# The last two chunks of tokens cut at 448 and 256 columns in place of 320 and 384, in a fused attention and expert kernel

## The chip, the cores and the metric

The kernel runs on one core of a Trainium2 chip. The metric is the device time of one execution in microseconds. The trace names the engines PE (matmul), PEld (its weight loads), DVE, ACT, POOL and SP (which issues most DMAs); each works through its own queue in order, and semaphores hold an instruction until what it needs is there.

## The reference

```python
# attention: q, k, v of (4, 4, 1088, 32); S1, S2 of (8, 32)
phi = lambda x: outer(S1 @ x, S2 @ x)               # 64 features per row
kv, z = phi(k).T @ v, phi(k).sum(rows)
attn = (phi(q) @ kv) / (phi(q) @ z + 1e-6)
x = attn, heads side by side                        # (4352 tokens, 128)
# four experts: w1 of (4, 128, 1024), w2 of (4, 1024, 128)
p = domain_probs / (domain_probs.sum(-1) + 1e-9)
out = sum over e of p[:, e:e+1] * (relu(x @ w1[e]) @ w2[e])
```

All inputs and the output are float32.

## The kernel before

**Two halves that overlap.** The attention produces the token matrix x piece by piece (generator `front`, cut into units of up to 576 tokens by `UNITS`); the experts consume it in ten chunks of tokens, `CHUNKS`, of 128, 448, six of 512, then 320 and 384 columns. A chunk has 32 slots (four experts of eight blocks of 128 hidden units); the first has 16. The main loop (L1468) goes through the slots in order and, between the work of the slots, calls `work`, which advances the attention by a few pieces. Before a chunk begins its tokens must be there; the last unit of the attention is complete before the next-to-last chunk starts.

**How many pieces a call of `work` advances** is decided while the program is built: a rate from the tokens still missing, a credit, and two estimates of the engines' load (`vector_time`, `scalar_time`, with LIMIT and SLOT).

**One slot.** Float32 accuracy is made of three float32r products, so a block takes six PE passes of the chunk's width: wa and wb into an h bank (`opening`, L1126 to L1137), then wd into the same bank one slot later (`third`, L1154), after ACT has scaled the bank in place (L1135); then va, vb and vd into an o bank (`second`, five slots later by LAG, four in the last expert by LAG_TAIL; the vd passes are dealt out later still by `pay`). Nearly all of these passes are issued from one helper, `swap`, so they stand under L949 and are told apart by their operands. Between the two groups the hidden block is split: ACT makes ha (L1184) and, for some blocks, hc (L1186), DVE makes hb (L1191), and POOL or DVE finishes hc (L1213, L1214, L1193, L1206). A letter per block (`MAKERS`, one row per chunk; `MAKER_TAIL` for the very last expert) says which engine does what. In the letters A and N, ACT has two operations behind the scaling, in most others one.

**One expert.** After its eighth block ACT scales the o bank (L1268). When the last vd pass is in, `gather` multiplies by the expert's gate (L1396; L1394 for the first expert) and adds to the chunk's total (L1397), which sets the o bank free. There are two o banks, so the expert after the next needs it. `next_gates` then has SP load a gate (L429), a tile of 128 partitions by the chunk's width, into the buffer that has come free. After the fourth expert `turn_back` transposes the total and stores it. Six more PSUM banks are shared by everything else.

**The last chunk** ends differently: the blocks with letters X and T of its last expert are plain (`w_tail`, and L1343 after ACT's relu in L1170 and the gate in L1171), `last_sums` adds what was gathered (L1329, L1332, one addition per 128 columns), and `last_rows` turns the result by matmuls (L1343, L1346), copies it out of PSUM and stores it in two DMAs (L1353).

**SP's queue** carries the loads and stores of both halves in program order. Early on (slot 5) it stores the gates, then loads the first GATES of them, then issues `load_k(1)` and `load_v(1)` for the next batch (L1530 to L1534).

```python
    TAIL = 4
    LAG_TAIL = 4
    DEALT = (0, 1, 1, 2, 2, 2)
    PLACES += [(START[m], START[m + 1], ring, (m - 3) % 3 * CW) for m in range(3, NC)]
```

The first of these is the number of plain blocks whose weights are loaded for the last expert, the last says where in the ring of tokens a chunk lies.

Of the kernel before, what the change touches and what calls it, by code (L numbers as in the profile page):

```python
# [24 lines left out]
def kernel(  # L25
# [24 lines left out]
    nc = tc.nc  # L50
    scalar_copy = lambda to, of: nc.scalar.activation(to, of, ACTF.Copy)

    P = 128
    HP = 64
    B, H, S, D = q.shape
# [10 lines left out]
    CW = 512  # L66
    GE = 160
    LAG = 5
    GATES = 2
    BUFFERS = (7, 6, 13)  # L70
    HA, HB, HC = BUFFERS
    WHOLE = 5
# [6 lines left out]
    LAG_TAIL = 4  # L79
    DEALT_TAIL = (1, 1, 2)  # L80
    DEALT = (0, 1, 1, 2, 2, 2)
    LIMIT = 1300.0
    LIMIT_A = 1e9
    SLOT_A = 1500.0
    SLOT = 1600.0
    PLAIN = (2,)
    TOKENS_AT = 16
    AHEAD = 13
    TOKENS = 6
    LEAD = 6  # L90
    SETTLE = 1
    SPREAD = 2
    XD_BY = 'PPVVPPPVPP'
    Q_BY = 'PVPPPPVVPVVVPVVPPP'
    O_BY = 'AAAA'
    FETCH = 8
    HOLD = (3, 1)
    DELAY = 0
# [7 lines left out]
    TOKENS_BY = "VV"  # L106
    UNITS = [[P, 448, 512], [576, 512], [576, 512], [576, 512]]

    CHUNKS = [P, 448] + [512] * 6 + [320, 384]
    NC = len(CHUNKS)  # L110
    START = [sum(CHUNKS[:m]) for m in range(NC + 1)]
    assert all(sum(u) == S for u in UNITS) and sum(CHUNKS) == B * S

# [32 lines left out]
    def load_k(b):  # L146
        kn[b] = lpool.tile([P, S], F32, tag="rows", name="kn")
        load_rows(k, b, kn[b])
# [29 lines left out]
    def xpieces(name, t):  # L178
        return mpool.tile([P, 3, CW], t, tag="x", name=name)
# [235 lines left out]
    def parts(m):  # L415

        c, end, at = START[m], START[m] + CHUNKS[m], 0
        while c < end:
            n = min(end, (c // S + 1) * S) - c
            yield c // S, c % S, n, at  # L420
            c, at = c + n, at + n
# [3 lines left out]
    def load_gates(m, experts):  # L425
        for e in experts:
            gate[m, e] = mpool.tile([P, CW], F32, tag="gate", bufs=GATES, name="gate")
            for b, c, n, at in parts(m):
# [99 lines left out]
    def key_sum(b, p, kv, t0=0, n=NT):  # L528
        for t in range(t0, t0 + n):
            both(  # L530
                kv[:, 256 * p : 256 * p + 2 * (D + 1)],
                kps[b][:, t, p, :],
                vx[:, t, 2 * p : 2 * p + 2].rearrange("p h d -> p (h d)"),

                start=(p == t == 0),
                stop=(t == NT - 1),
                skip_group_check=True,
            )
# [275 lines left out]
    def queries_by_dram(b, c, n):  # L814

        for _ in range(FETCH):
            yield
# [7 lines left out]
        if c + n < S:  # L825
# [3 lines left out]
            if c + n + m == S and b < B - 1:  # L829
                load_k(b + 1)  # L830
        for _ in range(14 - FETCH):
            yield
# [118 lines left out]
    def token_parts(m):  # L951

        n = CHUNKS[m]
        t = xpieces("xs", F32R)
# [11 lines left out]
    def start():  # L966
# [37 lines left out]
        for t0, n0 in ((0, 4), (4, 5)):  # L1004
            for p in range(2):
                key_sum(b, p, kv, t0, n0)
        qp = [xd_ for xd_ in (mpool.tile([P, CW], F32, tag="gate", bufs=GATES, name="qp") for _ in range(2))]
        for x in range(2):
# [24 lines left out]
    def front():  # L1033
        for b in range(B):
            if b:
                yield from keys(b)
                if b + 1 < B:
                    load_v(b + 1)
            c = 0
            for n in UNITS[b]:  # L1040
                if b or c:
                    yield from queries(b, c, n)
                c += n
# [5 lines left out]
    slots = [("pair", 0, e, f) for e in range(E) for f in range(NP)]  # L1049
    for m in range(1, NC):  # L1050
        slots += [("one" if m > 1 or FB * e + k >= MIXED else "mixed" if FB * e + k >= WHOLE else "whole", m, e, k) for e in range(E) for k in range(FB)]
    first_slot = {m: min(i for i, s in enumerate(slots) if s[1] == m) for m in range(NC)}
    per_chunk = {m: sum(s[1] == m for s in slots) for m in range(NC)}
# [40 lines left out]
    def opening(i):  # L1094

        kind, m, e, k = slots[i]
        n = CHUNKS[m]
        if kind == "pair":
# [121 lines left out]
    def second(i):  # L1220
# [25 lines left out]
        elif kind == "one":  # L1246
# [19 lines left out]
            elif k == FB - 1:  # L1266
                if O_BY[e] == "A":
                    nc.scalar.activation(o[:, 0:n], o[:, 0:n], ACTF.Copy, scale=1.0 + R12)  # L1268
# [133 lines left out]
                yield  # L1402
            turn_back(m, total.pop(m)[:, 0:n])

    vector_time, scalar_time = [0.0], [0.0]

    def on_vector(inst):

        if inst.engine == mybir.EngineType.DVE and inst.outs:
            n = 1  # L1410
            for _, d in list(inst.outs[0].ap)[1:]:
                n *= d
            vector_time[0] += n / 0.96 + 80
        elif inst.engine == mybir.EngineType.Activation and inst.outs and type(inst).__name__ != "InstDMACopy":
            n = 1
            for _, d in list(inst.outs[0].ap)[1:]:
                n *= d
            scalar_time[0] += n * 0.834 + 50

    start()  # L1420
    nc.push_inst_callback(on_vector)
    pieces = front()
    done, credit = [0], [0]

    def piece():
        done[0] += 1
        next(pieces, None)


    needed, columns, count = [0] * NC, UNITS[0][0], 0  # L1430
    for b in range(B):
        count += 17 if b else 0
        for n in UNITS[b] if b else UNITS[0][1:]:
            count, columns = count + (20 if count else 18), columns + n
            for m in range(NC):
                if columns - n < START[m] + CHUNKS[m] <= columns:
                    needed[m] = count
    for i in range(3):
        begun_hp[i] = psum(ps_h, "h")
        half_columns(i, begun_hp[i], 0)  # L1440
# [25 lines left out]
        due.setdefault(first_slot[1] + HOLD[1] if held else i + (LAG_TAIL if final(*s[1:3]) else lag[s[0]]), []).append(i)  # L1466
    i = 0
    while i < len(slots) or i <= max(due) or owed:  # L1468
        vector_time[0] = max(0.0, vector_time[0] - (SLOT * CHUNKS[slots[i][1]] / CW if i >= first_slot[1] and i < len(slots) else 900.0))
        scalar_time[0] = max(0.0, scalar_time[0] - (SLOT_A * CHUNKS[slots[i][1]] / CW if i >= first_slot[1] and i < len(slots) else 900.0))  # L1470
        if i < len(slots):
            kind, m, _, _ = slots[i]
            at = i - first_slot[m]
            while have[0] < START[m] + CHUNKS[m]:
                piece()

            gone = START[m] + CHUNKS[m] * at / per_chunk[m]
            left = lambda c: START[c] - (CHUNKS[c - 1] * AHEAD / per_chunk[c - 1] if c > 1 else 0) - gone
            rate = CHUNKS[m] / per_chunk[m] * max(
                [0] + [(needed[c] + (LEAD if c > 1 else 4) - done[0]) / left(c) for c in range(m + 1, NC) if left(c) > 0]  # L1480
            )

            def work(share):

                if not first_slot[1] <= i < first_slot[1] + 4:
                    credit[0] = min(credit[0] + rate * share, 3)
                while credit[0] >= 1 and vector_time[0] < LIMIT and scalar_time[0] < LIMIT_A:
                    credit[0] -= 1
                    piece()

            opening(i)
            if kind == "pair":
                work(0.5)
        for j in due.get(i, ()):
            second(j)
        if SETTLE:
            settle()
        third(i - DELAY if i < len(slots) else i)
        if not SETTLE:
            settle()  # L1500
        pay()
        next(ending, None)
        if i < len(slots):
            work(0.5 if kind == "pair" else 1)
            if at == per_chunk[m] - AHEAD and 0 < m < NC - 1:
                while have[0] < START[m + 1] + CHUNKS[m + 1]:
                    piece()
            for gen in to_part.get(i, ()):
                next(gen, None)
            if m == NC - 2 and at == per_chunk[m] // 2:  # L1510
                while have[0] < B * S:
                    piece()
                w2_tail = load_tail()
                one = dram.tile([P, P], F32, name="one")
                nc.sync.dma_start(one[:, :], unit[:, 0:P])
                nc.sync.dma_start(bass.AP(one.tensor, one.offset, [[P + 1, P], [1, 1]]), unit[:, P : P + 1])
                nc.sync.dma_start(unit[:, 0:P], one[:, :])
            if i == first_slot[1] + 10:
                for j in range(3):
                    load_plain(j)  # L1520
            for j in range(3, len(plain_order)):
                if i == first_slot[2] + 8 * (j - 3) + 7:
                    load_plain(j)
            if i == first_slot[4]:
                unit = cpool.tile([P, P + 1], F32, tag="dp", name="unit")
                nc.gpsimd.memset(unit[:, 0:P], 0.0)
                nc.gpsimd.memset(unit[:, P : P + 1], 1.0)
            if i == 2:
                gate_quotients()
            elif i == 5:  # L1530
                store_gates()
                next_gates(GATES)
                load_k(1)
                load_v(1)  # L1534
        if i == 2:

            made_hp[3] = psum(ps_h, "h")
            for c in (0, HP):
                half_columns(3, made_hp[3], c)
        i += 1  # L1540
    for _ in ending:
        pass
    last_rows(NC - 1, unit)
    nc.pop_inst_callback()

# [1 line left out]
_INS = ["q", "k", "v", "S1", "S2", "moe_domain_probs", "moe_w1", "moe_w2"]  # L1547
# [26 lines left out]
```

## Time and profile before

| | us |
|---|---|
| median of 3 runs | 425.93 (425.80 to 425.94) |
| the profiled execution | 426.43 |
| its span, first to last instruction | 424.70 |
| busy: PE, ACT, DVE, POOL | 416.5, 382.0, 357.0, 355.3 |

The granted TensorE clock is 1.00 over the whole span. A busy time is the union of the records of an engine. Records of one engine overlap (an operation's record ends after the next one has started), so the distance between two starts, not the length of a record, says how fast an engine gets through its queue. A window view gives the busy time of each engine in a stretch, and the chain is the sequence of work that ended last, followed back from the end of the window.

### The profile page before, as it was taken

The page shows a single profiled execution, that of the slowest core. Times are in us where ns is not written, and L with a number is a line of the kernel's source. Part 1 is how long each engine was busy: PE and PEld are TensorE (multiplying, and loading weights), DVE is VectorE, ACT ScalarE, POOL GpSimd, SP SyncE. Part 2 cuts the span into 40 slices and gives each one's busy share as a digit, 9 for nine tenths or more (in the row PEclk, how much of TensorE's full clock was granted, in tenths as well). Part 3 has the DMA queues.
Part 4 walks back from the last instruction along what each step waited for, and adds up shares of the span by engine and source line. Part 5 has one row for each costly group of instructions (what it writes and reads, how often), then busy time and mean ns, then how long its engine had stood idle before and what let it go on. Part 6 is the DMA issues. An engine that isn't in the chain of part 4 may idle for free.

```text
span 424.7 us, 8812 instructions
## 1 busy us (share of the span) xinstructions
PE 416.5 (98%) x2819; PEld 351.7 (83%) x2819; DVE 357.0 (84%) x626; ACT 382.0 (90%) x818; POOL 355.3 (84%) x371
## 2 busy tenths in 40 slices
PE   9999999999999999999999999999999999999996
PEld 7886677888888887878888887878778888989995
DVE  5869999888798896898799996896897878879894
ACT  4368898999999998999999988998999999999992
POOL 6441468999999999997999998897989999799992
PEclk9999999999999999999999999999999999999999
DMA  6925250446512401643602415212621221040110
GB/s 194 320 60 130 47 145 2 98 80 158 165 40 51 126 27 44 136 99 95 176 5 61 114 26 117 61 33 62 161 32 23 41 75 35 23 82 27 34 38 19
DMA packets 57646, 34.66 MB, mean 82 GB/s; under 512 B 34945, under 2 KB 50689, under 8 KB 57601
## 3 DMA queue, kind: packets, MB, share of 16 engines
q1 hardware_dynamic: 57504, 34.01, 31.5%
q8 instruction: 22, 0.36, 0.4%
q14 instruction: 24, 0.19, 0.2%
q10 hardware_dynamic: 96, 0.10, 0.1%
HBM read 28.94 MB, written 5.15 MB: 80 GB/s over the span
## 4 chain that ended last, share of the span: by engine, by line
PE 82%; ACT 8%; DVE 4%; issue 3%; DMA 2%; SPq 0%; DVEq 0%; ACTq 0%
PE o L949 36%; PE h L949 36%; PE h L318 6%; ACT ha L1184 3%; ACT h L1135 3%; ACT hc L1186 2%; PE h L497 1%; DMA qn_first<-in_q_dram 1%; PE o L318 1%; DMA kn<-in_k_dram 1%; PE h L1121 1%; DVE hb L1191 1%; DVE o L1396 1%; SPq L171 0%; DVE qs L637 0%
## 5 line engine op out<-in xcount | busy, mean ns | idle before, releaser
L1214 POOL TENSOR_TENSOR hc<-hb,hc 128x512 fp32r<-128x512 f32 (+3 forms) x204 | 252.5, 1260 | 23.1 <-DVE hb L1191 16.9
L1191 DVE SCALAR_TENSOR_TENSOR hb<-h,ha 128x512 fp32r<-128x512 f32 (+3 forms) x266 | 166.8, 641 | 48.9 <-ACT hc L1186 16.9
L1135 ACT ACTIVATE h<-h 128x512 f32<-128x512 f32 (+3 forms) x283 | 166.3, 588 | 4.1 <-PE h L949 3.5
L1184 ACT ACTIVATE ha<-h 128x512 fp32r<-128x512 f32 (+3 forms) x252 | 148.8, 590 | 2.0 <-PE h L949 0.4
L949 PE MATMUL h<-xs,wd 128*128 128x512 f32 (+3 forms) x283 | 109.2, 386 | 1.3 <-ACT h L1135 0.5
L949 PE MATMUL h<-xs,wa 128*128 128x512 f32 (+3 forms) x283 | 105.5, 373 | 0.0
L949 PE MATMUL h<-xs,wb 128*128 128x512 f32 (+3 forms) x283 | 102.5, 362 | 0.0
L949 PE MATMUL o<-ha,va 128*128 128x512 f32 (+3 forms) x266 | 96.8, 364 | 1.1 <-DVE total L1397 1.1
L949 PE MATMUL o<-hb,vb 128*128 128x512 f32 (+3 forms) x266 | 96.6, 363 | 0.0
L949 PE MATMUL o<-hc,vd 128*128 128x512 f32 (+3 forms) x262 | 79.7, 366 | 0.2
L1186 ACT ACTIVATE hc<-h 128x512 fp32r<-128x512 f32 (+3 forms) x124 | 74.1, 598 | 0.0
L949 PEld LDWEIGHTS h<-xs,wd 128*128 128x128 f32 x283 | 53.3, 188 | 19.8 <-ACT h L1135 11.6
L1213 POOL TENSOR_SCALAR hc<-ha 128x512 fp32r<-128x512 f32 (+3 forms) x80 | 57.4, 717 | 8.1 <-ACT ha L1184 1.6
L949 PEld LDWEIGHTS h<-xs,wa 128*128 128x128 f32 x283 | 53.5, 189 | 9.5 <-issue 2.9
L949 PEld LDWEIGHTS h<-xs,wb 128*128 128x128 f32 x283 | 53.5, 189 | 5.7 <-issue 0.6
L949 PEld LDWEIGHTS o<-ha,va 128*128 128x128 f32 x266 | 50.3, 189 | 7.5 <-PE h L949 2.3
L949 PEld LDWEIGHTS o<-hc,vd 128*128 128x128 f32 x262 | 48.5, 189 | 7.9 <-issue 1.6
L949 PEld LDWEIGHTS o<-hb,vb 128*128 128x128 f32 x266 | 50.3, 189 | 5.5 <-DVE hb L1191 0.2
L1193 DVE SCALAR_TENSOR_TENSOR hc<-ha,hb 128x512 fp32r<-128x512 f32 (+2 forms) x41 | 36.2, 882 | 1.4
L1268 ACT ACTIVATE o<-o 128x512 f32<-128x512 f32 (+3 forms) x33 | 18.4, 557 | 0.0
L1397 DVE TENSOR_TENSOR total<-o,total 128x512 f32<-128x512 f32 (+3 forms) x26 | 16.9, 650 | 0.9
L1396 DVE TENSOR_TENSOR o<-o,gate 128x512 f32<-128x512 f32 (+3 forms) x26 | 16.8, 647 | 0.3 <-PE o L949 0.3
(161 smaller groups left out, 405.2 us busy)
## 6 DMA issues: line engine op xcount, KB each, us to landing
w_sb<-in_moe_w_dram SPq DMA_DIRECT2D x8, 512.0 KB
gate<-gates SPq DMA_DIRECT2D x16, 256.0 KB
kn<-in_k_dram SPq DMA_DIRECT2D x4, 544.0 KB
gate<-gates SPq DMA_DIRECT2D x8, 224.0 KB
qs<-rows SPq DMA_DIRECT2D x6, 288.0 KB
qs<-rows SPq DMA_DIRECT2D x12, 144.0 KB
qn<-in_q_dram SPq DMA_DIRECT2D x3, 544.0 KB
vx<-in_v_dram SPq DMA_DIRECT2D x48, 32.0 KB
```

Source lines behind the costliest of these rows:

```text
L318: nc.tensor.matmul(out(s), weights(s), moving(s), **flags)
L949: nc.tensor.matmul(to, weights, t, **flags)
L1135: nc.scalar.activation(g, g, ACTF.Copy, scale=1.0 + R12)
L1184: nc.scalar.activation(ha, g, ACTF.Relu, scale=NEAR)
L1186: nc.scalar.activation(hc, g, ACTF.Relu, scale=NEAR * R12)
L1191: nc.vector.scalar_tensor_tensor(out=hb, in0=g, scalar=0.0, in1=high, op0=ALU.max, op1=ALU.subtract)
L1193: nc.vector.scalar_tensor_tensor(out=hc, in0=high, scalar=-R12, in1=rest, op0=ALU.mult, op1=ALU.add)
L1213: nc.gpsimd.tensor_scalar(out=hc, in0=high, scalar1=R12, scalar2=1.0, op0=ALU.mult, op1=ALU.mult)
L1214: nc.gpsimd.tensor_tensor(out=hc, in0=rest, in1=both_, op=ALU.subtract)
L1268: nc.scalar.activation(o[:, 0:n], o[:, 0:n], ACTF.Copy, scale=1.0 + R12)
L1396: nc.vector.tensor_tensor(out=o[:, 0:n], in0=o[:, 0:n], in1=g, op=ALU.mult)
L1397: nc.vector.tensor_tensor(out=total[m][:, 0:n], in0=o[:, 0:n], in1=total[m][:, 0:n], op=ALU.add)
```

## The change

The next-to-last chunk becomes 448 columns wide in place of 320, the last one 256 in place of 384; together they are 704 as before. Three gate buffers are held in place of two. The rule by which a call of `work` decides how many pieces to advance is replaced by a string of digits, one for each call. Everything that the width of the last chunk sets goes with it: its slots, its output, the number of additions in L1332 and of matmuls in L1343 and L1346.

```diff
-    GATES = 2
+    GATES = 3
...
-    LIMIT = 1300.0
-    LIMIT_A = 1e9
-    SLOT_A = 1500.0
-    SLOT = 1600.0
...
-    LEAD = 6
...
+    PIECES = "01101101110110003011011011101101000012121212121111220022111110212102211121022111211101111100030111021111100021111111111111003011110210211100301111021111110012111100210211002111111020111100121111021101110030111101201011000210110020101100201010100000000000000000000000000000000000000000000000000000000000000000000000000000"
...
-    CHUNKS = [P, 448] + [512] * 6 + [320, 384]
+    CHUNKS = [P, 448] + [512] * 6 + [448, 256]
...
-            gone = START[m] + CHUNKS[m] * at / per_chunk[m]
-            left = lambda c: START[c] - (CHUNKS[c - 1] * AHEAD / per_chunk[c - 1] if c > 1 else 0) - gone
-            rate = CHUNKS[m] / per_chunk[m] * max(
-                [0] + [(needed[c] + (LEAD if c > 1 else 4) - done[0]) / left(c) for c in range(m + 1, NC) if left(c) > 0]
-            )
-
-            def work(share):
-
-                if not first_slot[1] <= i < first_slot[1] + 4:
-                    credit[0] = min(credit[0] + rate * share, 3)
-                while credit[0] >= 1 and vector_time[0] < LIMIT and scalar_time[0] < LIMIT_A:
-                    credit[0] -= 1
+            def work():
+
+                steps[0] += 1
+                for _ in range(int(PIECES[steps[0] - 1])):
                     piece()
```

What is left out removes the two estimates and their callback, and the arguments of the calls of `work`.

More of the change, by code (lines that the diff above doesn't have):

```diff
@@ L1403, in gather @@
             turn_back(m, total.pop(m)[:, 0:n])
[L1405 to L1418, printed above, removed]
     start()
-    nc.push_inst_callback(on_vector)
     pieces = front()
-    done, credit = [0], [0]
+    steps = [0]
     def piece():
-        done[0] += 1
         next(pieces, None)
[L1430 to L1437, printed above, removed]
     for i in range(3):
@@ L1468 @@
     while i < len(slots) or i <= max(due) or owed:
-        vector_time[0] = max(0.0, vector_time[0] - (SLOT * CHUNKS[slots[i][1]] / CW if i >= first_slot[1] and i < len(slots) else 900.0))
-        scalar_time[0] = max(0.0, scalar_time[0] - (SLOT_A * CHUNKS[slots[i][1]] / CW if i >= first_slot[1] and i < len(slots) else 900.0))
         if i < len(slots):
@@ L1492 @@
             if kind == "pair":
-                work(0.5)
+                work()
         for j in due.get(i, ()):
@@ L1503 @@
         if i < len(slots):
-            work(0.5 if kind == "pair" else 1)
+            work()
             if at == per_chunk[m] - AHEAD and 0 < m < NC - 1:
@@ L1543 @@
     last_rows(NC - 1, unit)
-    nc.pop_inst_callback()
 _INS = ["q", "k", "v", "S1", "S2", "moe_domain_probs", "moe_w1", "moe_w2"]
```

## The prediction

> **What bounds the kernel now.** I read the page's busy times first, then the windows view cut at the starts of the last two chunks (the first 320-column pass of L949 starts at 353.29, the first 384-column one at 383.68), then the chain of waits in those windows, and last the timeline for the distance between starts.
>
> ```profile
> PE 416.5 (98%) x2819; PEld 351.7 (83%) x2819; DVE 357.0 (84%) x626; ACT 382.0 (90%) x818; POOL 355.3 (84%) x371
> ```
>
> PE is never long idle, so a change pays only through work taken from PE, gaps in front of PE, or what comes after its last pass. But a busy PE says little: a 320-column matmul is recorded as 0.30 us long while the next one starts 0.136 us later, so a small gap hides under the overlap. I therefore count starts.
>
> ```profile
> core 0: us, PE busy (x) PEld busy (x) DVE busy (x) ACT busy (x) POOL busy (x), PEclk, DMA share, GB/s
> 305.80:353.30 47.50, 47.31 (x241) 39.49 (x241) 39.92 (x63) 47.05 (x94) 44.02 (x39) 1.00 0.23 52
> 353.30:383.70 30.40, 29.81 (x194) 27.58 (x193) 24.92 (x50) 30.23 (x86) 26.67 (x33) 1.00 0.21 45
> 383.70:418.60 34.90, 34.80 (x210) 33.16 (x209) 31.07 (x59) 32.58 (x81) 30.42 (x35) 1.00 0.12 28
> 418.60:424.70 6.10, 2.19 (x19) 2.00 (x17) 1.72 (x5) 0.56 (x2) 0.00 (x0) 1.00 0.09 32
> ```
>
> In the 320-column chunk (second row) ACT is busy 30.23 of 30.40 us; in the 384-column chunk it has 2.3 us to spare. The chain through those two windows, in the same order, says the same: only in the first does it leave PE often.
>
> ```profile
> by line: PE o L949 28.6%; PE h L949 22.2%; issue 10.6%; DVE hb L1191 9.8%; ACT ha L1184 9.5%; ACT hc L1186 7.2%; ACT h L1135 7.0%; DVE hc L1193 2.6%; DVE o L1396 2.0%; ACT xs L886 0.5%; DVEq L1362 0.2%; DVE total L1397 0.1%; DVEq L1191 0.1%
> by line: PE h L949 47.1%; PE o L949 42.6%; ACT ha L1184 4.0%; ACT h L1135 2.9%; issue 2.1%; ACT hc L1186 1.9%; ACT hid L1197 0.1%; ACTq L1135 0.0%
> ```
>
> **The two rates.** In stretches without a gap, the timeline has PE starts 0.2157 us apart at 512 columns (345.89 to 347.40, seven passes), 0.1623 at 384 (394.77 to 396.88, thirteen) and 0.136 at 320 (364.04 to 366.08, fifteen). That is one line, 0.000415 us a column plus 3 ns, and gives 0.189 at 448 and 0.109 at 256. ACT's closest starts are about 0.475, 0.37 and 0.32 us apart at 512, 384 and 320 columns: 0.427 at 448 and, carried on, 0.267 at 256. So a pass has almost no fixed part, while an ACT operation has some 50 ns that do not shrink.
>
> ```profile
> 361.88 0.44 ACT L1184 ACTIVATE ha<-h 128x320 fp32r<-128x320 f32 x1
> 362.20 0.45 ACT L1186 ACTIVATE hc<-h 128x320 fp32r<-128x320 f32 x1
> 362.51 0.46 ACT L1135 ACTIVATE h<-h 128x320 f32<-128x320 f32 x1
> ```
>
> These three are ACT's unit of work here: its records are 0.44 to 0.46 long, its starts 0.32 apart.
>
> **Part 1, PE's own work.** The next-to-last chunk costs 32 slots x 6 passes = 192 passes of its width. The last costs 96 into h, 28 blocks x 3 passes and two plain float32 blocks at the price of four passes each: 188 up to the end of w_tail. 128 columns move from the second to the first: 192 x 0.0531 = +10.20, 188 x 0.0531 = -9.98, so +0.2 us. Instruction counts do not change, except behind the last pass.
>
> **Part 2, the chunk that grows.** Before, in 353.3 to 383.7 PE starts 169 passes of 320 (23.0 us) and 24 of 512 (5.2): 28.2 of 30.4 us, 2.2 lost. The gaps between starts name them. 0.25 at 358.56 and 0.57 at 366.08 are first va passes waiting until L1397 has released an o bank. About 1.0 us in all at 372.8, 379.2 and 380.2 is a wd pass waiting for ACT's h; about 0.5 at 373.9 and 381.4 is an hc pass just behind ACT's o copy. ACT's load explains the last two: the maker letters give 84 operations, 85 with the xs split, x 0.32 = 27.2 us against 192 x 0.136 = 26.1 of PE. At 448 the same 85 cost 36.3 and PE 36.3: the 1.1 us of excess is gone, and the time from wb to the wd that needs ACT's result, eight passes at least, grows from 1.09 to 1.51 us. The bank waits should go, since the bank is needed five and thirteen slots into the chunk and the last 512-column gathers ahead of it do not grow. Bounds for what stays lost: 0.3 (only gaps that no rate explains) and 2.2 (nothing improves). The nearest row is the 512-column chunk just ahead, 47.5 us with ACT 47.05 busy, whose gaps between starts come to about 1.6 of 47.5; scaled to 37 us, 1.2; with the bank waits gone I take 1.0. Change: -1.2 (0 to -1.9). What moves with it: xs of this chunk is 448 wide at the end of the chunk ahead (+0.1 us on ACT and DVE, +0.3 on POOL), and the other one as much narrower.
>
> **Part 3, the chunk that shrinks.** Before: 180 passes and the plain blocks at 384 (30.5) and 25 passes of 320 (3.4) are 33.9 of 34.9 us, 1.0 lost. ACT: 75 x 0.373 = 28.0 against 30.5. At 256: 75 x 0.267 = 20.0 against 188 x 0.109 = 20.6, so ACT's 8% of spare time becomes 3%, and the eight passes between wb and wd are 0.87 us, against about 0.75 that ACT needs to return h (a 0.27 us matmul, 0.38 as the 128x256 rows of L1116 last, two hand-overs of some 0.05). In the last group of eight, which runs with LAG_TAIL 4, the o bank is wanted two slots after the last hc pass; two gathers of about 0.43 and one L1191 of 0.42 no longer fit, 0.4 against 0.145 now. Bounds for the loss: 0.5, if all of it stays hidden, and 3.3, if to the 1.0 of now each slot with three ACT operations (eight of 32) adds 0.15 (0.80 of ACT against six passes), the three o copies 0.8 and the bank wait 0.3. Nearest row: the 320-column chunk, 1.4 without its bank waits where ACT stood 4% above PE. With ACT 3% below, but less room to wait in, I take 1.7: change +0.7 (-0.5 to +2.3).
>
> [...]
>
> **Part 4, behind the last pass.**
>
> ```profile
> 418.79 0.57 DVE L1329 TENSOR_TENSOR h<-h,gate 128x384 f32<-128x384 f32 x1 [0.62 <-PE h L949]
> 419.39 0.86 DVE L1332 TENSOR_TENSOR hid<-h,total 128x128 f32<-128x128 f32 x3
> 420.42 0.68 ACT L51 ACTIVATE ob<-h 128x128 f32<-128x128 f32 x2 [3.57 <-PE h L1346]
> 421.13 0.60 SPq L1353 DMA_DIRECT2D out_dram<-ob  x1
> ```
>
> This is a chain: product with the gate, one addition per 128 columns, L1346, the last copy, the store. At 256 columns L1329 is 0.13 shorter (1.04 ns a column, from 0.57 at 384 and 0.69 for L1396 at 512) and one of three additions goes (0.24 between starts). The four L1343 records less (0.43) lie beside it. The store moves a third less in the 0.9 us in which the DMA view has it moving; the rest of its 3.6 us is issue and completion: -0.2. Together -0.6 (-0.35 to -0.85).
>
> **Part 5, no time.** PIECES: following the old credit rule call for call through the 320 calls of work gives the same 320 digits, 215 pieces, so the order of the attention work stays, and since all of it is done before the next-to-last chunk the new widths do not meet it. GATES: each load still follows one gather and waits for that gather's product, as the waits of SP's queue show before too (L429 on L1396, 127.6 us). The third buffer puts one more load in front of load_k(1), 0.34 us of SP at 33.9; kn is first read at 52.97, and the vx loads that follow end at 48.8 while their reader starts at 72.3. Without that cover it would cost the 0.34 and its 224 KB.
>
> **Sum.** +0.2 - 1.2 + 0.7 - 0.6 = -0.9 us. The profiled execution took 426.43 (span 424.70 and 1.73 around it), 0.5 above the median of the runs, 425.93; what is saved is within one execution, so I take it off the median: 425.0.
>
> **Rivals.** (A) Better: the wider chunk keeps only 0.3 to 0.6, the narrow one runs as densely as the 384 one does from 390 to 411: -1.7 + 0 + 0.2 - 0.6, some 423.8, at best 422.9. For it: letters with fewer ACT operations (75 against 84) sit in the narrow chunk, as its rate wants. Chance 0.20. (B) The two chunks trade evenly, +0.8 more in the last one: 425.9. Chance 0.10. (C) Slower: ACT becomes the bound of the last chunk, with the full 3.3 lost there, while the wider chunk sheds only its bank waits: +2.3 - 0.8 + 0.2 - 0.6 = +1.1, 427.0, and 427.8 where it sheds nothing. It decides if ACT's starts at 256 columns lie more than 20.6/75 = 0.274 us apart or h returns later than 0.87 us after wb; my 0.267 and 0.75 are near. Chance 0.24, and 0.01 more for the price of the page above: about +6.7 where 0.7 stood, 431. (D) A pass of 256 columns is held to its weight load: the loads are recorded as 189 ns, and 188 x 0.080 = 15 us would be 440. Against it: loads overlap at 320 columns, and L497's records, each with a 128x128 load of its own, start 0.112 apart (16 in 1.95 us). Chance 0.03.
>
> **How the numbers follow.** The forecast has 0.42. A measurement of this kernel can tell about 0.2%, 0.85 us, from no change, so its own range, 424.2 to 425.7, lies on both sides of 425.08: 0.30 of it counts as faster, 0.12 as same. Faster 0.30 + 0.20 = 0.50; same 0.12 + 0.10 = 0.22; slower 0.24 + 0.01 + 0.03 = 0.28. The range goes from the best of (A), 422.9, to the far end of (C), 427.8.
>
> **What would show it.** Right: starts 0.189 and 0.109 apart in dense stretches; the 448 chunk without the two long va gaps and about 38.1 us long (37.1 of passes, the 24 of 512 among them); about 27 us from the first 256-column pass to the last w_tail pass; 5.5 us behind it. Wrong: wd passes waiting for L1135 in most slots of the last chunk, L949 starts at 256 further apart than 0.11 with no engine to blame, gaps in the 448 chunk like those of the 320 one, or any stage before 345 us that moves.

## The result and the profile after

The changed kernel takes 427.16 us (median of nine, 426.72 to 427.49) against 425.93 (425.70 to 426.58): a ratio of 1.0028, with a 95% interval of 1.0018 to 1.0038. It is 1.2 us slower, where 0.9 us faster was forecast. The execution that was profiled took 427.38 us with a span of 425.30, so 2.08 around the span; before it was 426.43, 424.70 and 1.73. Lines behind the edit stand four lower than before: the passes of L949 are L945 now, L1135 is L1131, L1184 and L1186 are L1180 and L1182, L1191 and L1193 are L1187 and L1189, L1396 and L1397 are L1392 and L1393. In the experiments some of them shift by a few lines more.

The page's busy times after:

```profile
PE 417.3 (98%) x2813; PEld 352.2 (83%) x2813; DVE 358.1 (84%) x625; ACT 383.1 (90%) x817; POOL 355.6 (84%) x371
```

The windows after, cut at the same places (the first pass of 448, the first of 256, the first L1339):

```profile
core 0: us, PE busy (x) PEld busy (x) DVE busy (x) ACT busy (x) POOL busy (x), PEclk, DMA share, GB/s
305.70:353.15 47.45, 47.20 (x240) 39.48 (x239) 39.86 (x63) 47.00 (x94) 44.02 (x38) 1.00 0.20 51
353.15:391.60 38.45, 38.30 (x194) 35.56 (x192) 30.81 (x51) 38.27 (x86) 33.56 (x34) 1.00 0.16 39
391.60:419.70 28.10, 27.31 (x209) 25.97 (x209) 26.77 (x59) 25.85 (x81) 23.88 (x35) 1.00 0.10 24
419.70:425.30 5.60, 1.77 (x13) 1.38 (x11) 1.34 (x4) 0.28 (x1) 0.00 (x0) 1.00 0.07 23
```

Up to the start of the second row (353.15, before 353.29) nothing has moved but the whole sequence, by 0.14 us to the front. The next-to-last chunk is 8.06 us longer than before, the last one 6.81 shorter, what lies behind it 0.51 shorter: together with the 0.14 the span grew by 0.60.

Read the third row across. By their records PE, DVE, ACT and POOL are all busy for 24 to 27 of 28.1 us. Before, in the last chunk, DVE had 3.8 us to spare (31.07 of 34.90); now it has 1.3, less than ACT's 2.2. The chain through the two chunks, in the same order, puts DVE ahead of ACT as well:

```profile
by line: PE o L945 43.9%; PE h L945 41.0%; issue 7.3%; DVE hb L1187 4.0%; DVE xs L887 2.3%; DVE o L1392 1.6%; DVE total L1393 0.1%; DVE hc L1189 0.1%
by line: PE h L945 22.9%; PE o L945 22.1%; DVE hb L1187 16.0%; issue 13.9%; ACT ha L1180 8.2%; ACT h L1131 5.7%; DVE total L1393 3.8%; DVE o L1392 3.2%; ACT hc L1182 2.6%; DVE hc L1189 1.3%; DVE ha L1184 1.2%; DVE hc L1202 0.9%; DVEq L1187 
```

The wide chunk's chain is now nearly all PE, as hoped. But the last chunk's, 90% PE before and without a single DVE entry, spends 26% on DVE's L1187, L1393, L1392, L1189, L1184 and L1202 and 17% on ACT.

**How the loss is counted below.** "Gaps" are the distances between PE starts beyond the pass's own (0.110 us at 256 columns, 0.189 at 448), where they exceed it by 0.03, added up; the plain float32 passes of w_tail, which start twice as far apart (0.216 at 256 columns, 0.322 at 384), count as no gap. Before: 2.39 in the next-to-last chunk and 0.99 in the last. After: 1.46 and 2.66. Of the 2.66, 1.18 stands in front of va passes, 0.49 in front of vb, 0.37 at hc passes, 0.35 at wa and 0.27 at wd.

Where the largest of them comes from can be read in the timeline after, around one of the three va waits, and at three operations of DVE's L1189 (start, length, engine, line, operation, what ended the idle time before it):

```profile
401.14 0.83 DVE L1189 SCALAR_TENSOR_TENSOR hc<-ha,hb 128x256 fp32r<-128x256 f32 x1
...
402.22 0.62 DVE L1392 TENSOR_TENSOR o<-o,gate 128x448 f32<-128x448 f32 x1
...
402.87 0.62 DVE L1393 TENSOR_TENSOR total<-o,total 128x448 f32<-128x448 f32 x1
...
403.11 0.28 PE L945 MATMUL h<-xs,wb 128*128 128x256 f32 x1
...
403.64 0.35 PE L945 MATMUL o<-ha,va 128*128 128x256 f32 x1 [0.26 <-DVE total L1393]
...
403.94 0.40 POOL L1209 TENSOR_SCALAR hc<-ha 128x256 fp32r<-128x256 f32 x1
404.19 0.43 DVE L1189 SCALAR_TENSOR_TENSOR hc<-ha,hb 128x256 fp32r<-128x256 f32 x1
...
405.79 0.73 POOL L1210 TENSOR_TENSOR hc<-hb,hc 128x256 fp32r<-128x256 f32 x1
405.85 0.95 DVE L1189 SCALAR_TENSOR_TENSOR hc<-ha,hb 128x256 fp32r<-128x256 f32 x1
```

The second to fifth rows: an expert of the wide chunk is still being gathered when the narrow chunk is under way. Its two DVE operations are 448 wide and take 0.62 each, while six passes of the narrow chunk take 0.66. The o bank comes free at 403.49; the va pass that wants it starts 0.53 after the pass in front of it (403.11) instead of 0.11, so the gap is 0.42. The same happens behind the passes at 396.28 (0.33) and, with gathers 256 wide, at 414.63 (0.43). The first row, an L1189 of 0.83 us, stands ahead of this gather in DVE's queue, with one hb operation between them; run 3 shows that most of the 0.42 hangs on it.

The last four rows: two operations of one line and one shape, 0.43 and 0.95 long. Each started while POOL was in an operation, L1209 or L1210, and ended 0.28 after it. So its record holds a wait for POOL, which the width of the chunk does not shorten by itself. The groups view has the mean of all nine, before:

```profile
L1191 DVE SCALAR_TENSOR_TENSOR hb<-h,ha 128x384 fp32r<-128x384 f32 x28 | 14.9, 549 | 1.9 <-PE h L949 0.6 <-ACT ha L1184 0.5 <-POOL hc L1214 0.4
L1193 DVE SCALAR_TENSOR_TENSOR hc<-ha,hb 128x384 fp32r<-128x384 f32 x9 | 6.6, 737 | 0.3
```

and after:

```profile
L1187 DVE SCALAR_TENSOR_TENSOR hb<-h,ha 128x256 fp32r<-128x256 f32 x28 | 10.7, 412 | 0.2
L1189 DVE SCALAR_TENSOR_TENSOR hc<-ha,hb 128x256 fp32r<-128x256 f32 x9 | 7.2, 802 | 0.3
```

The hb operation shrank from 549 to 412 ns with the width; L1189, whose two operands both lie in SBUF, went from 737 to 802. Note also the last column: DVE's hb operations idled 1.9 us before them, waiting for PE and ACT, and now 0.2. DVE hardly waits for the others any more.

Behind the last pass the timeline after has:

```profile
419.90 0.43 DVE L1325 TENSOR_TENSOR h<-h,gate 128x256 f32<-128x256 f32 x1 [0.31 <-PE h L945]
420.37 0.61 DVE L1328 TENSOR_TENSOR hid<-h,total 128x128 f32<-128x128 f32 x2
...
421.39 0.28 ACT L51 ACTIVATE ob<-h 128x128 f32<-128x128 f32 x1 [2.75 <-PE h L1342]
...
421.99 0.61 SPq L1349 DMA_DIRECT2D out_dram<-ob  x1
```

One addition less, a product that is 0.14 shorter, and the store is issued 2.29 us after the first L1339 instead of 2.53.

### The profile page after: what moved, and what is told of

Read it like the earlier page. It is cut to its first block, busy times and chain, and to the rows that moved or that the text cites. A ratio compares the mean times of both kernels' runs of the same rounds, so it can differ in the third digit from the quotient of the medians.

```text
span 425.3 us, 8795 instructions
## 1 busy us (share of the span) xinstructions
PE 417.3 (98%) x2813; PEld 352.2 (83%) x2813; DVE 358.1 (84%) x625; ACT 383.1 (90%) x817; POOL 355.6 (84%) x371
## 4 chain that ended last, share of the span: by engine, by line
PE 80%; DVE 7%; ACT 5%; issue 4%; DMA 3%; POOL 0%; SPq 0%; DVEq 0%; ACTq 0%
PE o L945 35%; PE h L945 34%; PE h L314 7%; ACT h L1131 2%; ACT ha L1180 2%; DVE hb L1187 2%; PE h L493 1%; PE o L314 1%; DMA xd<-y 1%; PE h L1117 1%; ACT hc L1182 1%; DVE o L1392 1%; DMA gate<-gates 1%; DMA ring<-xd 1%; DVE total L1393 0%
## 5 line engine op out<-in xcount | busy, mean ns | idle before, releaser
L1210 POOL TENSOR_TENSOR hc<-hb,hc 128x512 fp32r<-128x512 f32 (+2 forms) x204 | 254.6, 1269 | 25.0 <-DVE hb L1187 18.7
L1187 DVE SCALAR_TENSOR_TENSOR hb<-h,ha 128x512 fp32r<-128x512 f32 (+2 forms) x266 | 167.0, 642 | 49.5 <-ACT hc L1182 18.4
L1131 ACT ACTIVATE h<-h 128x512 f32<-128x512 f32 (+2 forms) x283 | 167.1, 590 | 4.4 <-PE h L945 3.8
L1180 ACT ACTIVATE ha<-h 128x512 fp32r<-128x512 f32 (+2 forms) x252 | 150.1, 596 | 2.3 <-PE h L945 0.6
L945 PE MATMUL h<-xs,wd 128*128 128x512 f32 (+2 forms) x283 | 109.5, 387 | 1.0 <-ACT h L1131 0.5
L945 PE MATMUL h<-xs,wa 128*128 128x512 f32 (+2 forms) x283 | 105.5, 373 | 0.0
L945 PE MATMUL h<-xs,wb 128*128 128x512 f32 (+2 forms) x283 | 102.6, 362 | 0.0
L945 PE MATMUL o<-ha,va 128*128 128x512 f32 (+2 forms) x266 | 97.1, 365 | 1.6 <-DVE total L1393 1.4
L945 PE MATMUL o<-hb,vb 128*128 128x512 f32 (+2 forms) x266 | 96.8, 364 | 0.1
L945 PE MATMUL o<-hc,vd 128*128 128x512 f32 (+2 forms) x262 | 80.1, 368 | 0.2
L1182 ACT ACTIVATE hc<-h 128x512 fp32r<-128x512 f32 (+2 forms) x124 | 75.6, 609 | 0.0
L945 PEld LDWEIGHTS h<-xs,wd 128*128 128x128 f32 x283 | 53.3, 188 | 19.7 <-ACT h L1131 11.6
L1209 POOL TENSOR_SCALAR hc<-ha 128x512 fp32r<-128x512 f32 (+2 forms) x80 | 55.9, 699 | 8.2 <-ACT ha L1180 1.7
L945 PEld LDWEIGHTS h<-xs,wa 128*128 128x128 f32 x283 | 53.5, 189 | 9.5 <-issue 2.9
L945 PEld LDWEIGHTS h<-xs,wb 128*128 128x128 f32 x283 | 53.6, 189 | 5.7 <-issue 0.6
L945 PEld LDWEIGHTS o<-ha,va 128*128 128x128 f32 x266 | 50.3, 189 | 8.2 <-PE h L945 2.7
L945 PEld LDWEIGHTS o<-hc,vd 128*128 128x128 f32 x262 | 48.5, 189 | 8.0 <-issue 1.4
L945 PEld LDWEIGHTS o<-hb,vb 128*128 128x128 f32 x266 | 50.3, 189 | 5.6 <-DVE hb L1187 0.5
L1189 DVE SCALAR_TENSOR_TENSOR hc<-ha,hb 128x512 fp32r<-128x512 f32 (+2 forms) x41 | 37.7, 919 | 1.4
L1393 DVE TENSOR_TENSOR total<-o,total 128x512 f32<-128x512 f32 (+2 forms) x26 | 17.0, 655 | 0.9
L1392 DVE TENSOR_TENSOR o<-o,gate 128x512 f32<-128x512 f32 (+2 forms) x26 | 17.0, 652 | 0.2 <-PE o L945 0.2
```

What stands on the lines that cost most here:

```text
L945: nc.tensor.matmul(to, weights, t, **flags)
L1131: nc.scalar.activation(g, g, ACTF.Copy, scale=1.0 + R12)
L1180: nc.scalar.activation(ha, g, ACTF.Relu, scale=NEAR)
L1182: nc.scalar.activation(hc, g, ACTF.Relu, scale=NEAR * R12)
L1187: nc.vector.scalar_tensor_tensor(out=hb, in0=g, scalar=0.0, in1=high, op0=ALU.max, op1=ALU.subtract)
L1189: nc.vector.scalar_tensor_tensor(out=hc, in0=high, scalar=-R12, in1=rest, op0=ALU.mult, op1=ALU.add)
```

## The experiments

Theory and rivals after the result: **(D)** DVE is what the last chunk waits for, through L1189 and through the gathers that hold the o banks; **(A)** ACT is, as rival C of the prediction had it; **(O)** the two o banks themselves; **(S)** the string of digits or the third gate buffer costs the time, and the widths nothing. Ratios are to the kernel before with 95% intervals; "last chunk" is the time from the first 256-column pass to the first L1339, 28.10 in the changed kernel. The profiled execution of each is used for the stages.

**1. Undo the widths alone** (the string and GATES = 3 stay).

```diff
-    CHUNKS = [P, 448] + [512] * 6 + [448, 256]
+    CHUNKS = [P, 448] + [512] * 6 + [320, 384]
```

> The changed kernel with the last two chunks back at 320 and 384 columns; three gate buffers and the string of pieces stay. Both theories put the whole loss into the widths, so the time should be that of the kernel before, 425.9 us, within 0.4. If the gate buffer or the string costs anything, it shows here as time above 426.4.

Measured: 1.0003 (0.9994 to 1.0012). The two chunks take 30.40 and 34.90 us again, with gaps of 1.02 in the last. In these two chunks the widths carry the whole of it.

**2. The changed kernel with two gate buffers.**

```diff
-    GATES = 3
+    GATES = 2
```

> The changed kernel with two gate buffers as before. Both theories: no change, 427.1 within 0.3, unless the last gate, which POOL reads some 3.5 us after its load could start, comes late: then a wait of L1167 for it and up to 1 us more. It also shows whether the third buffer is what sets the 0.2 us between span and time that the run with the old widths had more than the kernel before.

Measured: 1.0031 (1.0019 to 1.0043), last chunk 28.11, both chunks 66.55 as with three. The third buffer neither costs nor saves anything that shows. With run 1, (S) falls.

**3. L1189 left out in the last chunk.**

```diff
+            left_out = m == NC - 1 and maker(m, e, b) == "V"
+            hc = near[0] if left_out else mpool.tile(...)
+            near[0] = hc
...
-            if by == "V":
+            if left_out:
+                pass
+            elif by == "V":
...
+    near = [None]
```

> The changed kernel; in the last chunk the nine blocks with letter V leave out their second DVE operation (L1189, mean 802 ns, 7.2 us in all) and use the third operand of the block ahead instead, so that part of the computation is changed. Theory 1 (DVE holds the last chunk: hb and the gathers come late, and with them the o banks): the last chunk loses some 1.5 to 2 us of its stalls, 425.4 us. Rival (ACT's fixed part per operation holds it): nothing to gain, 427.0 us, within 0.4.

Measured: 1.0012 (1.0004 to 1.0021), last chunk 27.41, gaps 2.00. DVE's nine operations, 7.2 us of records, are worth 0.7 us to PE, less than half of what theory 1 had. The waits of va at 396 and 414 (0.40 and 0.48 with the vb gap behind them) stay, and they are gathers, not L1189. The one shown above, behind the pass at 403.11, falls from 0.42 to 0.11, and a wait of vb at 398.67 (0.28) is gone: there L1189 had held up the gather and the hb operation that came after it in DVE's queue.

**4. ACT's second operation left out** in the last chunk's blocks A, D and N.

```diff
+            spared = m == NC - 1 and by in "ADN"
-            if by in "AD":
+            if by in "AD" and not spared:
...
-                if by == "N":
+                if spared:
+                    whole = high
+                elif by == "N":
...
-                nc.gpsimd.tensor_tensor(out=hc, in0=rest, in1=both_, op=ALU.subtract)
+                nc.gpsimd.tensor_tensor(out=hc, in0=rest, in1=high if spared else both_, op=ALU.subtract)
```

> The changed kernel; in the last chunk the letters A, D and N leave out ACT's second operation (nine operations, some 2.4 us of ACT's queue) and POOL or DVE read ha in its place, so that part of the computation is changed; the number of operations on DVE and POOL stays. Theory 1 (DVE): at most 0.3 us, 426.9. Rival (ACT): 1.5 to 2 us, 425.4.

Measured: 1.0017 (1.0007 to 1.0026), last chunk 28.05, gaps 2.64. The windows of this and the run before and of run 8, in this order (columns as in the windows above):

```profile
391.37:419.42 28.05, 26.80 (x208) 25.87 (x208) 26.81 (x59) 24.09 (x72) 23.85 (x35) 1.00 0.10 24
```
```profile
391.50:418.91 27.41, 27.01 (x208) 25.88 (x207) 21.10 (x50) 25.50 (x81) 23.32 (x35) 1.00 0.10 24
```
```profile
391.13:417.37 26.24, 26.24 (x209) 25.74 (x208) 20.72 (x50) 23.65 (x72) 23.17 (x35) 1.00 0.11 25
```

ACT lost 1.8 us of busy time (24.09 against 25.85) and the chunk 0.05. The gap in front of wd fell from 0.27 to 0.10, but those in front of va and vb rose, to 1.56 and 0.57: what ACT no longer held, DVE did. The ratio lies 0.0011 under that of the changed kernel, with intervals that overlap, and of the 0.3 us by which the profiled span is shorter most lies ahead of the two chunks (the wide one starts at 352.92 instead of 353.15). (A), alone, falls.

**5. A third o bank in the last chunk**, taken from the h banks for two of its experts.

```diff
+        if m == NC - 1:
+            return psum(ps_h, "h") if e in (0, 3) else psum(ps_o, f"o{(e + 1) % 2}")
...
+            given_back(o)
```

> The changed kernel with a third o bank in the last chunk, taken from the six h banks for its first and its last expert, so that no expert's first va pass waits for the gather of the expert two before. These waits are 0.40, 0.50 and 0.50 us in the trace. Theory 1, with the gathers as the place where DVE's lateness reaches PE: 426.1 us (1.4 us of waits go, some 0.4 come back as waits for hb). Theory 1 with hb itself as the place: 426.9. Rival (ACT): 426.8, since ACT's backlog meets PE a little later.

Measured: 1.0024 (1.0014 to 1.0033), last chunk 27.99, gaps 2.55. No va pass waits for a gather any more. The time has gone elsewhere, as its timeline shows:

```profile
398.45 0.19 PEld L945 LDWEIGHTS h<-xs,wa 128*128 128x128 f32 x1 [0.86 <-DVE hb L1189]
398.45 0.38 PE L945 MATMUL h<-xs,wa 128*128 128x256 f32 x1 [0.59 <-DVE hb L1189]
```

L1189 is the hb operation here. A wa pass waits until DVE has read the block that holds its h bank: the start is 0.75 us late in this one place, for three va waits removed. The edit also leaves the h passes with one bank fewer while the third o bank is held; this run does not tell how much of the new wait is that.

**6. Three and five together.**

> Both earlier edits of the last chunk together: the second DVE operation of the nine V blocks left out (that part of the computation is changed) and a third o bank. Theory 1: with DVE's queue short the gap before wa, 0.75 us, that came up when the bank was added does not come up, and the waits for the o bank that stayed when the operations were left out go as well: the gaps of the last chunk fall from 2.7 to about 1.1 us, 425.6. If the two waits have causes of their own, no more than one of the two gains shows: 426.4.

Measured: 1.0003 (0.9993 to 1.0012), last chunk 27.04, gaps 1.62. The bank alone gave 0.11 and L1189 alone 0.69; together they give 1.06. That lies between the two forecasts: the gaps did not fall to 1.1, but more than one of the two gains shows. Gaps of 0.69 stay in front of wa and 0.55 at hc passes.

**7. The vd passes dealt out earlier,** so that the gather comes earlier; in the changed kernel, and in the kernel before from one chunk earlier on (its edit has `m >= NC - 2 or m == NC - 3 and e > 1`).

```diff
-                owed.append([0, m, e, o[:, 0:n], later, DEALT])
+                owed.append([0, m, e, o[:, 0:n], later, (0, 2, 3, 3) if m == NC - 1 or m == NC - 2 and e > 1 else DEALT])
```

> The changed kernel; the vd passes of the last two experts of the 448-column chunk and of the first three of the last chunk are dealt 0, 2, 3, 3 a slot in place of 0, 1, 1, 2, 2, 2, so that the gather is queued two slots earlier. Theory 1 in its first form (the o bank is handed over too late for the narrow slots): the va waits of the last chunk, 1.4 us with what follows them, go, 426.1 us. Theory 1 in its second form (DVE is late with everything): the wait turns up at the next thing DVE releases, 426.9. Rival (ACT): no change, 427.1.

> The kernel before with vd passes dealt 0, 2, 3, 3 from the third expert of the last 512-column chunk on. The waits of va for an o bank in the 320-column chunk (0.25 and 0.57 us) should go: 425.3 us. If ACT, which is busy 30.2 of 30.4 us there, takes the place of them, no change: 425.9.

Measured: 1.0031 (1.0020 to 1.0043) and, in the kernel before, 1.0060 (1.0046 to 1.0073). In the first the two chunks take 66.60 us against 66.55, 0.76 of it moved into the wide one. Its waits in the last chunk (engine, line and releaser; us in total, times, longest):

```profile
PEld h L945 <- ACT h L1131: 1.6, 5, 0.4
```

and those of the changed kernel there:

```profile
PE o L945 <- DVE total L1393: 0.7, 3, 0.3
...
PEld h L945 <- ACT h L1131: 0.3, 1, 0.3
```

The wait for the gather is gone, and wd waits for ACT instead, five times rather than once. In the kernel before, the last two chunks have, without and with the early dealing:

```profile
PEld h L949 <- ACT h L1135: 1.3, 4, 0.4
```
```profile
PEld h L949 <- ACT h L1135: 4.2, 13, 0.6
```

The vd passes that are dealt out late are the cover between wb and wd, under which ACT returns h. Taken out of there, they leave wd bare.

**8. All three out:** L1189, ACT's second operations and the third bank, that is 3, 4 and 5 together.

> The changed kernel with three edits of the last chunk: the second DVE operation of V blocks and ACT's second operation of A, D and N blocks left out (those parts of the computation are changed), and a third o bank. If what stays after the first two edits together (1.6 us of gaps, before wa and hc above all) is ACT's queue, it falls to 1.0 or less: 425.7 us. If it is latency that no queue explains, no change: 426.3.

Measured: 0.9970 (0.9957 to 0.9982), last chunk 26.24, gaps 0.82; its window is the third of the rows under run 4, where PE is busy 26.24 of 26.24 us. The 0.8 us from run 6 to this one are what ACT's operations cost once DVE and the bank are out of the way; on their own, in run 4, they were worth 0.05. So none of (D), (A), (O) is the bound alone. Counted by distances between starts, DVE's operations in the changed kernel's last chunk come to some 24 us and ACT's to some 23, against the 25.4 that PE's passes take without a gap (PE still has 25 passes of the wide chunk in this stretch, 4.7 us). These two are estimates from the trace: for DVE the 29.0 us of its 57 records, less the 0.08 by which its next start comes ahead of a record's end; for ACT 32 scalings at 0.30, 43 others at 0.265 and five of the wide chunk at 0.42. Neither queue is longer than PE's, both leave little room to be late in, and when one is relieved, waits on the other come up. POOL was relieved in no run; here it is still busy 23.17 us while PE's gaps are down to 0.82, so its own queue does not hold PE. Whether shorter POOL operations would shorten L1189 was not tried.

**9. Other cuts,** to see whether the wide chunk's relief can be had without the narrow one: 448, 384, 384 with the string of digits and with the old rule, and 448, 448, 448, 384 with the old rule.

```diff
-    CHUNKS = [P, 448] + [512] * 6 + [448, 256]
+    CHUNKS = [P, 448] + [512] * 5 + [448, 384, 384]
```

> The changed kernel with the last four chunks at 512, 448, 384 and 384 columns in place of 512, 512, 448 and 256; string of pieces and gate buffers stay. No chunk is narrower than 384, where the last chunk of the kernel before lost 1.0 us. If the losses come from narrow chunks: 2.4 us of the 320-column chunk become some 1.2, 425.0 us against 425.9 before. If the attention, which must now be complete 64 columns earlier, crowds the 448-column chunk: 426.5 or more.

> The kernel before, with its own rule for the pieces, and the last four chunks at 512, 448, 384 and 384 columns in place of 512, 512, 320 and 384. As the run with the string: 425.0 us if narrow chunks are what costs; the rule spreads the attention over the earlier chunks anew, which may give or take some tenths.

> The kernel before, with its own rule for the pieces, and the last six chunks at 512, 512, 448, 448, 448 and 384 columns in place of 512, 512, 512, 512, 320 and 384 (the first two of them stay). PE's work is the same. If losses fall with width and 448 is wide enough: 424.8 us. If a chunk's loss per operation is fixed, the sum over the chunks stays and so does the time, 425.9; if the attention's pieces fall worse, it is slower.

Measured: 0.9995 (0.9981 to 1.0009), 0.9996 (0.9982 to 1.0010) and 1.0016 (1.0002 to 1.0030). In the first, a next-to-last chunk of 384 columns takes 34.02 us and still has gaps of 2.23, against 2.39 at 320. The width from 320 to 384 does almost nothing for that chunk, while at 448 it had 1.46; why is not shown. The gains of 0.9 to 1.1 us that were expected of the three cuts did not come. No cut that was run, with the whole computation in it, beats the kernel before by more than can be measured.

## Why the prediction was wrong

**What held.** PE's starts are 0.11 apart at 256 columns (399.38, 399.49, 399.60, 399.71, 399.82) and 0.19 at 448, so rival D fell. ACT's closest starts behind most of its operations are 0.26 to 0.28 us apart at 256 (0.267 forecast) and 0.42 at 448; behind the scaling they are not, see part 2. Part 5 held: no stage ahead of 353 us moved by more than 0.24 us, and runs 1 and 2 show that neither the string nor the third buffer costs anything that can be measured. Part 4 was -0.51 against -0.6.

**Part 1** was +0.2. Without the gaps, the two chunks took 0.5 us more of passes (36.99 and 25.44 against 28.00 and 33.92), which holds the gaps too small to be counted.

**Part 2** was half right. The chunk took 38.45 us against 38.1, its gaps 1.46 against 1.0. ACT's excess shrank, but it had been sized by one distance for all operations. The two traces, before at 320 columns and after at 256, say otherwise:

```profile
362.51 0.46 ACT L1135 ACTIVATE h<-h 128x320 f32<-128x320 f32 x1
362.87 0.46 ACT L1184 ACTIVATE ha<-h 128x320 fp32r<-128x320 f32 x1
```
```profile
402.35 0.38 ACT L1131 ACTIVATE h<-h 128x256 f32<-128x256 f32 x1
402.65 0.38 ACT L1180 ACTIVATE ha<-h 128x256 fp32r<-128x256 f32 x1
402.92 0.39 ACT L1131 ACTIVATE h<-h 128x256 f32<-128x256 f32 x1
```

Behind the scaling (L1135, now L1131), of which a chunk has 32, ACT's next start comes 0.30, 0.355, 0.41, 0.46 and 0.515 us later at 256, 320, 384, 448 and 512 columns, some 0.04 more than behind L1184 (0.264, 0.317, 0.37, 0.424, 0.477). By these distances ACT had 28.2 us against PE's 26.1 in the 320-column chunk and has 37.2 against 36.3 at 448: an excess of 2.1 that fell to 0.9, not 1.1 that fell to nothing. So the fall was forecast about right, with part of the excess left. And "the bank waits should go" did not hold: one is left, 0.36 us with its follow-up at 368.82, and so are the gaps behind ACT's o copies, twice 0.25 at 379.0 and 388.5. Change in gaps: -0.93, where -1.2 was taken.

**Part 3 is the step that failed.** Gaps of 2.66 where 1.7 was taken: a change of +1.67 instead of +0.7. Three things in it were wrong, all of one kind.
- It set ACT's 20.0 us against PE's 20.6 and took the closeness of these two for the size of the stall. With 0.30 behind the scalings ACT's 75 operations are some 21.0, above PE and not 3% below it. And DVE was not costed at all. DVE had 31.07 us of work in that chunk before. With L1193's 6.6 left as they are, the rest scaled as the hb operation was (412/549), and 1.2 added for the nine operations of the wide chunk that reach into it (0.13 each), some 26 come out, and 26.77 there are: as near to PE, by records, as ACT's 25.85. Run 4 shows that ACT alone was not what the chunk waited for: without nine of its operations, some 2.4 us, it stood 10% below PE, and the chunk was 0.05 us shorter. Run 3 shows that L1189 was a part of it.
- It let DVE's gathers meet the o bank only in the last group of eight, for 0.4 us. That one was right in size (0.43 at 414.63). But the gathers that a narrow chunk meets first belong to the wide chunk ahead: 0.62 us for each of two operations, in slots of 0.66. One more wait, 0.33, comes from this, and with L1189 ahead of the gather a second one, 0.42, of which 0.11 stayed in run 3. Part 2 had said that the gathers ahead of the growing chunk "do not grow"; that its own then run into the shrinking one was not carried over to part 3.
- The bounds, 0.5 to 3.3, did hold the 2.66, since they were worked out from ACT's rate with some room; that they held is luck, as DVE's part was in neither but for one bank wait. The choice within them went by ACT's 3% of spare time, which was not there and was not what decided.

**The rivals.** C had the price (427.0) and not the mechanism. It said that ACT becomes the bound and is decided at 0.274 us between its starts; in the mean of its 75 operations they are 0.28 (21.0/75), so by that sign ACT did stand above PE. But ACT's relief alone brought 0.05 us, and the time came out at 427.16 all the same: with 2.66 of gaps in the narrow chunk where C had 3.3, 0.93 shed in the wide one where it had 0.8, more passes, and 0.3 us that no part had. The +6.7 us (431) that stands beside C with a chance of 0.01 is shown by no run: by the trace after, ACT's 75 operations come to some 21.0 us in that chunk, against 20.6 of PE's passes, and its gaps to 2.66.

**The sum, as measured:** +0.51 of passes, -0.93 and +1.67 of gaps, -0.51 behind, -0.14 ahead: +0.60 of span. The forecast for the same was -0.9. Of the 1.5 us between them part 3 is 1.0, parts 1 and 2 are 0.3 each, and the tail's 0.1 and the 0.14 ahead cancel.

**What stays open.** The medians differ by 1.2 us and the spans of several runs by about 0.8 (425.2 against 424.4 to 424.5). The other 0.3 lie outside the span: 1.73 us before and 2.04 after, in the middle of their runs. It follows neither the widths nor the buffers: run 1, with the old widths, has 1.97, run 2 has 1.91, run 3 has 1.78 (1.80 and 1.81 in the other two runs without L1189), the kernel before with early dealing 2.16. Nothing in the trace says what it is.

## What to carry to other kernels

When a stage is made narrower, list the work of every engine in it, not only of the one that was the bound, and look for operations whose length is set by something other than their width: here DVE's L1189, which ended 0.28 us after a POOL operation each time and took 802 ns in the mean at 256 columns, against 737 at 384. Work that a wide stage leaves behind lands in the narrow one and keeps its old size: here gather operations of 0.62 us, where six passes take 0.66. Take an engine's pace behind each kind of its operations, not behind the closest pair: ACT's next start came 0.30 us behind a scaling and 0.264 behind the operation that makes ha. And where the queues of several engines are nearly as long as that of the bound (here some 24 and 23 us by the estimates under run 8, against 25.4), reliefs can gain more together than their sum (0.7, 0.1 and 0.05 us alone, 1.9 together), so a relief that shows no gain does not clear its engine.

## What the hardware showed that was not expected

DVE's L1189, with both of its operands in SBUF, ended 0.27 to 0.29 us after a POOL operation in all nine cases of the last chunk, whatever its start: 398.98 + 0.79 against 398.77 + 0.73, 405.85 + 0.95 against 405.79 + 0.73, 410.71 + 0.99 against 410.69 + 0.73. The L1187 of the same shape, with one operand in PSUM, kept to 0.39 to 0.43 beside the same POOL operations. At 384 columns, in the kernel before, the nine L1193 ended 0.41 to 0.51 after a POOL operation. So what follows POOL's end shrinks with the width, and the wait ahead of it is set by when the operation meets POOL. All nine started after the POOL operation and ended after it. The price here is the rest of POOL's operation: the records are 0.80 us long in the mean, where the shortest of the nine took 0.43. What makes DVE wait there is not shown: L1189 and L1187 differ in their arithmetic as well as in where one operand lies, and no run changed one without the other.
